# The order of the output matmuls' halves in a fused Fourier-mixing and feed-forward kernel

## The chip, the cores and the metric

The kernel runs on one core of one Trainium2 chip. The metric is device time in microseconds (us) of one launch. The core has five engines that matter here: TensorE (PE in the profile; PEld is its weight load), VectorE (DVE), ScalarE (ACT), GpSimd (POOL) and SyncE (SP), which issues the stores of the result.

## The reference

```
x: (8, 3008, 256) float32
X   = real(fft(fft(x, axis=1), axis=2))        # 8 sequences, 3008 positions, 256 features
t   = X.reshape(24064, 256)
h   = maximum(t @ w_in, 0)                     # w_in: (256, 2048)
out = (h * h) @ w_out                          # w_out: (2048, 256), out: (24064, 256) float32
```

So a two-dimensional Fourier transform of each sequence, of which the real part is kept, and then a feed-forward layer with a squared ReLU.

## The kernel before

The transform over the features is folded into the input weights once (`gh`). The transform over the positions is done with fold steps on VectorE (symmetric and antisymmetric sums of the sequence) and matmuls with cosine and sine tables (L486), whose results ScalarE and VectorE write as the columns `zc` and `zs` (L491, L495, L502). One column of these stands for a pair of output rows, k and its mirror image, and so gives two rows of the hidden layer.

**Windows and steps.** The columns are cut into 25 windows: 240, 512, 376, 376, 512, 448, then 512 each and a last one of 360. For each window the main loop goes through 8 steps (`s`, 0 to 7); a step makes 256 of the 2048 hidden units, that is two chunks of 128, for all columns of the window. The result is `h2`, of 16 chunks x 2 x columns, in float16, with two buffers, since the window after it reads it.

A step has one of two forms. In a plain step `pq` computes the sum of the two parts into a PSUM tile `ph` (L739, L740), `square` lets ScalarE apply the ReLU into `h1` (L749) and VectorE, or in some steps ScalarE, square it into `h2` (L754 or L752); then `turn` (L745) changes the sign of one part in `ph`, and ReLU and square are done again for the mirror rows. In a halved step `half_q` (L764) computes one part alone, ScalarE copies it to `sn` (L772), `half_p` (L778) adds the other part, ScalarE copies that to `hd` (L780), and for a group of one or two steps VectorE makes both signs from the copies: L788 and L792, then L802, L803 (the ReLU) and L804 (the squares, into `h2`). `PLAN` says which steps of a window are halved and where ScalarE squares. Step 0 is plain in every window. `ph` has two buffers, `h1` three.

**The output matmuls.** While window w makes its `h2`, the output of window w-1 is computed from the other `h2`, in `ffn2_steps`. Its rows are cut into groups of 128 (8 groups for 512 columns). A group needs 16 matmuls of 128 x 128 x 256 (L625), one for each chunk of `h2`, accumulated in PSUM; two groups share one bank of 512 float32 (`po`, two banks). The work of one group is given as two jobs, `part(i, 0)` with chunks 0 to 7 and `part(i, 1)` with chunks 8 to 15. The job that ends the second group of a bank also has ScalarE evict it (L640) into `osb` (three buffers) and SyncE issue its stores (L605).

`spread` deals the list of jobs over the 8 steps, two jobs a step for 8 groups; `others` issues them between the first and the second matmuls of a step (between `pq` and `turn`, or `half_q` and `half_p`), in this order with the fold work and the matmuls of the transform (L486):

```
for j in at[s]: j()                   # fold work of a later sequence
for j in spread(f2, s, NST): j()      # output matmuls of the window before
for j in post[s]: j()
...                                   # z: matmuls with the tables, L486
```

The order on each engine is the order in which the program issues the instructions (a manual schedule); waits between the engines are put in from what each instruction reads and writes. So the job list of `ffn2_steps` alone decides at which step a chunk of the older `h2` is first read. At the end of step 5 (in most windows) ScalarE issues a small DMA (L586), and at the end of a window its counterpart (L588), which bring a row into all partitions for L788.

Of the kernel before, what the change touches and what calls it, by code (L numbers as in the profile page):

```python
# [8 lines left out]
F32 = mybir.dt.float32  # L9
# [6 lines left out]
P = 128  # L16
# [12 lines left out]
def kernel(  # L29
# [14 lines left out]
    nc = tc.nc  # L44
    B, S, D = x.shape
# [8 lines left out]
    NFC = F // P  # L54
# [62 lines left out]
    ps_o = ctx.enter_context(tc.tile_pool(name="ps_o", bufs=2, space=bass.MemoryType.PSUM))  # L117
    ps_z = ctx.enter_context(tc.tile_pool(name="ps_z", bufs=2, space=bass.MemoryType.PSUM))
# [65 lines left out]
    wout16 = const.tile([P, NFC, D], F16, name="wout16")  # L184
# [405 lines left out]
    def store(osb, p0, g0, m, minus, eng=nc.sync):  # L590

        for b, k0, kstep, n, c0 in runs:
            il, ih = max(g0, c0) - c0, min(g0 + m, c0 + n) - 1 - c0
            if minus and k0 in (0, H):
                il = max(il, 1)
            cnt = ih - il + 1
            if cnt <= 0:
                continue
            if minus:
                lo = p0 + (m - 1) - (c0 + ih - g0)  # L600
                row = b * S + S - (k0 + kstep * ih)
            else:
                lo = p0 + c0 + il - g0
                row = b * S + k0 + kstep * il
            eng.dma_start(  # L605
                out=bass.AP(tensor=out.tensor, offset=out.offset + row * D, ap=[[kstep * D, cnt], [1, D]]),
                in_=osb[lo : lo + cnt, :])

    def ffn2_steps(w, h2, tail=False):

        g0, wn = wins[w]
        groups = [(q, min(P, 2 * wn - q)) for q in range(0, 2 * wn, P)]
        jobs = []
        st = {}

        def part(i, hf):
            q, m = groups[i]
            j = 0 if tail else i % 2
            if tail and hf == 0 and i % 4 > 1:
                st["po"] = ps_z.tile([P, 512], F32, name="po", tag="pz")  # L620
            elif j == 0 and hf == 0:
                st["po"] = ps_o.tile([P, 512], F32, name="po", tag="po")
            po = st["po"]
            for fc in range(hf * 8, hf * 8 + 8):
                nc.tensor.matmul(po[0:m, j * D : (j + 1) * D], h2[:, fc, q : q + m], wout16[:, fc, :], start=(fc == 0), stop=(fc == NFC - 1))  # L625
            if hf == 1 and tail:

                osb = osp.tile([P, 2, D], F32, name="osb", tag="osb")
                nc.scalar.activation(osb[0:m, 0, :], po[0:m, j * D : (j + 1) * D], AF.Copy, bias=0.0, scale=HS * HS)
                nu = max(0, min(m, wn - q))  # L630
                if nu:
                    store(osb[:, 0, :], 0, g0 + q, nu, False)
                if nu < m:
                    store(osb[:, 0, :], nu, g0 + 2 * wn - q - m, m - nu, True, nc.scalar if i % 2 else nc.sync)
            elif hf == 1 and (j == 1 or i + 1 == len(groups)):
                osb = osp.tile([P, 2, D], F32, name="osb", tag="osb")
                for a, b in ((i - j, i),) if j == 0 or m == P else ((i - 1, i - 1), (i, i)):
                    mm = groups[b][1]
                    lo, hi = (a % 2) * D, (b % 2 + 1) * D
                    nc.scalar.activation(osb[0:mm].rearrange("p s d -> p (s d)")[:, lo:hi], po[0:mm, lo:hi], AF.Copy, bias=0.0, scale=HS * HS)  # L640
                for b in range(i - j, i + 1):
                    q1, m1 = groups[b]
                    nu = max(0, min(m1, wn - q1))
                    if nu:
                        store(osb[:, b % 2, :], 0, g0 + q1, nu, False)
                    if nu < m1:
                        store(osb[:, b % 2, :], nu, g0 + 2 * wn - q1 - m1, m1 - nu, True)

        for i in range(len(groups)):
            for hf in range(2):  # L650
                jobs.append(lambda i=i, hf=hf: part(i, hf))
        return jobs

    def spread(jobs, i, n):
# [34 lines left out]
    for w in range(NW):  # L689
        g0, wn = wins[w]  # L690
        h2 = h2p.tile([P, NFC, 2 * WN], F16, name="h2", tag="h2")
# [37 lines left out]
        for u in need[w + 1]:  # L729
            zu = z_steps(u)  # L730
            zj += [(zu, 1, 0), (zu, 0, 0), (zu, 1, 1), (zu, 0, 1)]
        f2 = ffn2_steps(*old) if old else []
        phs = {}

# [117 lines left out]
    for j in ffn2_steps(*old, tail=True):  # L852
        j()
# [30 lines left out]
```

## Time and profile before

| | |
|---|---|
| median of 3 runs | 620.15 us (620.01 to 624.33) |
| the profiled execution | 619.85 us, of which 618.1 us are the span of the program's instructions |
| PE busy | 584.0 us (94%) |
| PEld busy | 421.0 us (68%) |
| DVE busy | 503.7 us (81%) |
| ACT busy | 519.1 us (84%) |
| output matmuls (L625) | 3024, busy 363.9 us, mean row 273 ns |
| idle time of PE ahead of them | 14.6 us |

A row of the profile gives the line, engine and operation, what it writes and reads, its count, then busy time and mean duration, and last the idle time of its engine before it and who ended most of that. The rows of matmuls overlap, since they are pipelined. In the timeline a line has start, duration, engine and source line, and in brackets the idle time of the engine before it with the instruction that ended it.

### The profile page before, as it was taken

The numbers are of one execution on the slowest core, as the hardware profiler recorded it, in microseconds if no ns is written. First come the engines' busy times: TensorE is split into PE (matmuls) and PEld (weight loads), VectorE is DVE, ScalarE is ACT, GpSimd is POOL, SyncE is SP. The second block draws the span as 40 slices with busy tenths as digits, with TensorE's granted clock in tenths as the row PEclk, the third lists the DMA queues.
The fourth block names the chain that finished last, engine by engine and source line by source line (L and its number), as shares of the span: only waits on it lengthen the run. The fifth ranks groups of instructions, "written<-read, shape, count | busy, mean of one in ns | idle before, by whom it ended". The sixth has DMA issues, their size and how long they took to land.

```text
span 618.1 us, 11384 instructions
## 1 busy us (share of the span) xinstructions
PE 584.0 (94%) x4386; PEld 421.0 (68%) x4386; DVE 503.7 (81%) x742; ACT 519.1 (84%) x673; POOL 85.3 (14%) x125
## 2 busy tenths in 40 slices
PE   5899999999998999998999989999899999999996
PEld 2457776776676677766776767767677676776685
DVE  7887677686988987989889889898798797887980
ACT  7786787889898889988888888988889898998881
POOL 5352200102001022030011200403000020000000
PEclk9999999999999999999999999999999999999999
DMA  8936121363114433432154311552111221221112
GB/s 146 218 74 141 56 72 35 57 139 104 53 49 85 119 100 83 112 110 58 50 102 104 98 53 43 103 125 83 51 35 61 86 70 49 56 51 50 49 55 66
DMA packets 39591, 50.20 MB, mean 81 GB/s; under 512 B 4572, under 2 KB 33393, under 8 KB 39537
## 3 DMA queue, kind: packets, MB, share of 16 engines
q0 software_dynamic: 9344, 22.14, 17.8%
q1 hardware_dynamic: 26899, 24.44, 12.9%
q10 hardware_dynamic: 3294, 2.90, 2.1%
q8 instruction: 34, 0.56, 0.4%
q14 instruction: 20, 0.16, 0.1%
HBM read 36.29 MB, written 27.86 MB: 104 GB/s over the span
## 4 chain that ended last, share of the span: by engine, by line
PE 45%; DVE 29%; issue 10%; ACT 10%; DMA 4%; POOL 1%; ACTq 0%; DVEq 0%; SPq 0%; POOLq 0%
PE po L625 27%; DVE h L804 7%; DVE hd L803 5%; DVE hd L802 5%; ACT h L749 4%; PE ph L745 4%; PE ph L778 3%; PE ph L764 3%; PE ph L739 3%; PE ph L740 3%; DMA out_dram<-osb 3%; DVE hd L788 2%; DVE h L754 2%; ACT sn L772 2%; DVE sn L792 2%
## 5 line engine op out<-in xcount | busy, mean ns | idle before, releaser
L625 PE MATMUL po<-wout,h 128*128 128x256 f16 (+1 forms) x3024 | 363.9, 273 | 14.6 <-DVE h L804 9.8
L625 PEld LDWEIGHTS <-h 128*128 128x128 f16 (+1 forms) x3024 | 295.6, 98 | 89.1 <-DVE h L804 11.7
L749 ACT ACTIVATE h<-ph 128x1024 f16<-128x1024 f32 (+4 forms) x222 | 204.8, 951 | 34.0 <-PE ph L745 13.7
L754 DVE TENSOR_TENSOR h<-h 128x1024 f16<-128x1024 f16 (+4 forms) x159 | 97.5, 632 | 38.9 <-ACT h L749 36.9
L804 DVE TENSOR_TENSOR h<-hd 128x4096 f16<-128x4096 f16 (+7 forms) x50 | 100.0, 1999 | 1.3
L780 ACT ACTIVATE hd<-ph 128x1024 f16<-128x1024 f32 (+3 forms) x89 | 89.1, 1001 | 12.3 <-PE ph L778 11.8
L772 ACT ACTIVATE sn<-ph 128x1024 f16<-128x1024 f32 (+3 forms) x89 | 88.8, 998 | 0.0
L792 DVE TENSOR_TENSOR sn<-sn,hd 128x2048 f16<-128x2048 f16 (+7 forms) x50 | 53.9, 1078 | 39.6 <-ACT sn L772 37.4
L739 PE MATMUL ph<-zc,gh 128*128 128x512 f16 (+4 forms) x222 | 79.6, 361 | 1.1 <-ACT h L749 0.8
L740 PE MATMUL ph<-zs,gh 128*128 128x512 f16 (+4 forms) x222 | 79.6, 361 | 0.4 <-ACT zs L495 0.4
L640 ACT ACTIVATE osb<-po 128x512 f32<-128x512 f32 (+3 forms) x95 | 54.6, 578 | 21.3 <-PE po L625 17.2
L752 ACT ACTIVATE h<-h 128x1024 f16<-128x1024 f16 (+3 forms) x63 | 64.8, 1029 | 2.0
L802 DVE TENSOR_TENSOR hd<-hd,sn 128x2048 f16<-128x2048 f16 (+7 forms) x50 | 53.8, 1076 | 12.4 <-ACT hd L780 10.6
L745 PE MATMUL ph<-zs,gh 128*128 128x512 f16 (+4 forms) x222 | 61.0, 361 | 2.2 <-ACT h L749 1.2
L803 DVE TENSOR_SCALAR hd<-hd 128x4096 f16<-128x4096 f16 (+7 forms) x50 | 54.0, 1080 | 1.4
L778 PE MATMUL ph<-zc,gh 128*128 128x512 f16 (+3 forms) x178 | 51.7, 371 | 2.0 <-ACT sn L772 2.0
L788 DVE TENSOR_SCALAR hd<-eb,wv 128x512 f16<-128x512 f16 (+3 forms) x178 | 51.6, 346 | 0.8 <-DMA eb<-zr 0.8
L764 PE MATMUL ph<-zs,gh 128*128 128x512 f16 (+3 forms) x178 | 51.7, 372 | 0.0
L740 PEld LDWEIGHTS <-gh 128*128 128x128 f16 x222 | 21.6, 98 | 23.7 <-issue 2.5
L739 PEld LDWEIGHTS <-gh 128*128 128x128 f16 x222 | 21.6, 97 | 22.4 <-DVE zc L502 0.5
L764 PEld LDWEIGHTS <-gh 128*128 128x128 f16 x178 | 17.3, 97 | 20.0
L429 POOL COPY xt<-xt 128x2 f16<-128x2 f16 x16 | 3.7, 262 | 174.2 <-DVE xt L412 156.3
(121 smaller groups left out, 392.0 us busy)
## 6 DMA issues: line engine op xcount, KB each, us to landing
out_dram<-osb SPq DMA_DIRECT2D x77, 128.0 KB
xo<-in_x_dram POOLq DMA_DIRECT2D x7, 768.0 KB
scr<-ev POOLq DMA_DIRECT2D x8, 390.0 KB, 4.5
eb<-zr ACTq DMA_DIRECT2D x18, 128.0 KB
rb<-scr POOLq DMA_DIRECT2D x16, 130.0 KB
out_dram<-osb SPq DMA_DIRECT2D x12, 94.0 KB
w<-in_moe_w_in_dram POOLq DMA_DIRECT2D x2, 512.0 KB
wout<-in_moe_w_out_dram POOLq DMA_DIRECT2D x1, 1024.0 KB
```

Source lines behind the costliest of these rows:

```text
L625: nc.tensor.matmul(po[0:m, j * D : (j + 1) * D], h2[:, fc, q : q + m], wout16[:, fc, :], start=(fc == 0), stop=(fc == NFC - 1))
L739: nc.tensor.matmul(ph[:, a, 0:wn], gh[:, 0, f0 : f0 + P], zcw[:, 0:wn], start=True, stop=False)
L740: nc.tensor.matmul(ph[:, a, 0:wn], gh[:, 1, f0 : f0 + P], zsw[:, 0:wn], start=False, stop=True)
L745: nc.tensor.matmul(phs[s][:, a, 0:wn], gh[:, 2, f0 : f0 + P], zsw[:, 0:wn], start=False, stop=True, skip_group_check=True)
L749: nc.scalar.activation(h1[:, :, 0:wn], phs[s][:, :, 0:wn], AF.Relu)
L754: return [lambda: nc.vector.tensor_tensor(h2[:, 2 * s : 2 * s + 2, sg * wn : (sg + 1) * wn], hv, hv, op=ALU.mult)]
L764: nc.tensor.matmul(ph[:, a, 0:wn], gh[:, 1, f0 : f0 + P], zsw[:, 0:wn], start=True, stop=True)
L772: nc.scalar.activation(sns[g][:, i : i + 2, 0:wn], ph[:, :, 0:wn], AF.Copy, bias=0.0, scale=-2.0)
L780: nc.scalar.activation(hds[g][:, i : i + 2, 0:wn], ph[:, :, 0:wn], AF.Copy, bias=0.0, scale=1.0)
L802: lambda: nc.vector.tensor_tensor(rev_dim(hd[:, :, wn : 2 * wn], 2), hd[:, :, 0:wn], sn[:, :, 0:wn], op=ALU.add),
L803: lambda: nc.vector.tensor_scalar(out=hv, in0=hv, scalar1=0.0, scalar2=None, op0=ALU.max),
L804: lambda: nc.vector.tensor_tensor(h2[:, 2 * g[0] : 2 * g[-1] + 2, 0 : 2 * wn], hv, hv, op=ALU.mult),
```

## The change

For the output of every window after the third (`w > 2`) but the last, the job list begins with the first halves of groups 0 to 3 and then has their second halves; groups 4 and up stay as they were. With 8 groups, steps 0 and 1 then run the chunks 0 to 7 of the groups 0, 1 and 2, 3, steps 2 and 3 their chunks 8 to 15, and steps 4 to 7 one whole group each. Both banks of `po` are open meanwhile, each with two unfinished groups. [...] The open tile is kept per group (`st[i]`) instead of in one name. The other functions are unchanged; lines behind the edit are 1 to 4 higher.

```
+        four = w > 2 and not tail
...
             if tail and hf == 0 and i % 4 > 1:
-                st["po"] = ps_z.tile([P, 512], F32, name="po", tag="pz")
+                st[i] = ps_z.tile([P, 512], F32, name="po", tag="pz")
             elif j == 0 and hf == 0:
-                st["po"] = ps_o.tile([P, 512], F32, name="po", tag="po")
-            po = st["po"]
+                st[i] = ps_o.tile([P, 512], F32, name="po", tag="po")
+            po = st[i - j]
             for fc in range(hf * 8, hf * 8 + 8):
-                nc.tensor.matmul(po[0:m, j * D : (j + 1) * D], h2[:, fc, q : q + m], wout16[:, fc, :], start=(fc == 0), stop=(fc == NFC - 1))
+                nc.tensor.matmul(po[0:m, j * D : (j + 1) * D], h2[:, fc, q : q + m], wout16[:, fc, :], start=(fc == 0 and (j == 0 or not four or i > 3)), stop=(fc == NFC - 1), skip_group_check=(four and i < 4))
...
-        for i in range(len(groups)):
-            for hf in range(2):
-                jobs.append(lambda i=i, hf=hf: part(i, hf))
+        order = [(i, hf) for i in range(len(groups)) for hf in range(2)]
+        if four:
+            order = [(i, hf) for hf in range(2) for i in range(4)] + order[8:]
+        for i, hf in order:
+            jobs.append(lambda i=i, hf=hf: part(i, hf))
         return jobs
```

## The prediction

> **What bounds the kernel now.** I read the page first, then the waits of TensorE (PE), then the timeline around two window starts.
>
> ```profile
> PE 584.0 (94%) x4386; PEld 421.0 (68%) x4386; DVE 503.7 (81%) x742; ACT 519.1 (84%) x673; POOL 85.3 (14%) x125
> ...
> PEclk9999999999999999999999999999999999999999
> ...
> L625 PE MATMUL po<-wout,h 128*128 128x256 f16 (+1 forms) x3024 | 363.9, 273 | 14.6 <-DVE h L804 9.8
> ```
>
> ```profile
> PE po L625 <- DVE h L804: 9.8, 7, 2.0
> PE po L625 <- DVE h L754: 4.8, 6, 1.0
> ...
> ACT h L749 <- DVE h L754: 11.8, 12, 1.9
> ```
>
> PE is busy 94% of the 618.1 us span, and its clock row is full. Its largest idle group, 14.6 us, is the output matmul L625, and the waits view (total us, times, longest) says for whom: for VectorE (DVE) to finish the last squares, 7 times L804 and 6 times L754. Those are the waits that the change aims at. The last row belongs beside them: ScalarE (ACT) waits for the same squares, 12 times, because `h1`, which its relu (L749) writes, has three buffers and a square (L754) must have read one before it is written again. The steady part repeats every three windows, and the windows view of one such period (386.46 to 460.62) has, in us and PE, PEld, DVE, ACT:
>
> ```profile
> sum 74.16, PE 71.31 PEld 51.38 DVE 64.75 ACT 64.92 POOL 12.69; mean PE 23.77 PEld 17.13 DVE 21.58 ACT 21.64 POOL 4.23
> ```
>
> PE stands still for 2.85 us of 74.16. DVE and ACT have 9 us of idle time each, but not at the window starts. This is the start of the window at 435.77, from the timeline (start, duration, engine, line; the bracket is the idle time before it):
>
> ```profile
> 436.39 1.93 ACT L749 ACTIVATE h<-ph 128x1024 f16<-128x1024 f32 x2
> 436.63 1.25 PE L625 MATMUL po<-wout,h 128*128 128x256 f16 x10
> 438.23 1.23 DVE L804 TENSOR_TENSOR h<-hd 128x2048 f16<-128x2048 f16 x1
> 438.35 1.06 ACT L752 ACTIVATE h<-h 128x1024 f16<-128x1024 f16 x1
> 439.37 1.28 DVE L754 TENSOR_TENSOR h<-h 128x1024 f16<-128x1024 f16 x2
> 439.51 0.83 PE L625 MATMUL po<-wout,h 128*128 128x256 f16 x6 [1.63 <-DVE h L804]
> 440.18 0.59 PE L745 MATMUL ph<-zs,gh 128*128 128x512 f16 x2
> 440.81 1.02 ACT L749 ACTIVATE h<-ph 128x1024 f16<-128x1024 f32 x1 [1.40 <-PE ph L745]
> 441.73 1.02 ACT L772 ACTIVATE sn<-ph 128x1024 f16<-128x1024 f32 x1
> 442.80 0.59 PE L778 MATMUL ph<-zc,gh 128*128 128x512 f16 x2
> ```
>
> Ten matmuls of group 0 run, the eleventh (its chunk 10) waits for the L804 square, which ends at 439.46. A matmul's row overlaps the next one's: ten take 1.25 us with 0.273 for the last, so they start 0.109 apart. So the eleventh was due at 437.72 and started 1.79 us late, 0.16 more than its idle time; with that for each of the 13 waits, 16.7 us are lost in all. I call this an L804 start (seven). An L754 start (six), at 410.40:
>
> ```profile
> 411.26 1.69 PE L625 MATMUL po<-wout,h 128*128 128x256 f16 x14
> 412.63 1.29 DVE L754 TENSOR_TENSOR h<-h 128x1024 f16<-128x1024 f16 x2
> 413.54 1.02 ACT L749 ACTIVATE h<-ph 128x1024 f16<-128x1024 f32 x1 [1.85 <-DVE h L754]
> 413.97 0.39 PE L625 MATMUL po<-wout,h 128*128 128x256 f16 x2 [1.01 <-DVE h L754]
> 414.20 0.48 PE L486 MATMUL pz<-sin,od 128*128 128x376 f16 x2
> 414.61 0.59 PE L745 MATMUL ph<-zs,gh 128*128 128x512 f16 x2
> ```
>
> Here the L754 square ends the wait of PE, and it also ends a wait of ACT: relu 0 of the new window starts at 413.54, ends at 414.56, and L745, which needs it, starts 0.05 us later.
>
> **The change, part by part.** *Work.* No instruction is added or removed on any engine: the same 16 matmuls of L625 stand in each step of a full window, in another order. In the built program the waits for L804 and L754 leave the first step; the one for the last L804 stands at the third block of 16, two steps later (a step is 2.7 us: 442.80 to 445.47 below, L778 to L778). A DVE that is 1.8 us late is not late there, so the 16.7 us at L625 go. The order of a step's other instructions and all DMAs stays; of stores only the first set per window is issued later, after its eviction.
>
> *Where the stall goes, L754 starts.* PE would reach L745 1.18 us sooner, at 413.43, but relu 0 still ends at 414.56, since it waits for DVE and not for PE. The stall of 1.18 moves from L625 to L745; gain 0. The six together were 4.8 + 6 x 0.16 = 5.8 us.
>
> *L804 starts.* Relu 0 (the second of the two at 436.39) is done at 438.32, so L745 moves to 438.39. Next, the second relu (440.81) needs L745 and, in the built program, also the first of the two L754 at 439.37, by the buffers of `h1`. That one ends at 439.37 + 0.69 = 440.06. So this relu moves to 440.10 and no further: 0.71 us. L772 follows 0.92 us after it and ends at 442.04; L778 needs it and starts at 442.09 instead of 442.80, where PE without any wait would have it at 441.01. Gain 0.71 of 1.79; the other 1.08 stand at L778, a wait "ACT sn L772". The first and the last of the seven, same reading:
>
> ```profile
> 191.29 1.29 DVE L754 TENSOR_TENSOR h<-h 128x1024 f16<-128x1024 f16 x2
> 192.73 1.02 ACT L749 ACTIVATE h<-ph 128x1024 f16<-128x1024 f32 x1 [1.70 <-PE ph L745]
> ...
> 583.80 1.28 DVE L754 TENSOR_TENSOR h<-h 128x1024 f16<-128x1024 f16 x2
> 585.11 0.77 ACT L749 ACTIVATE h<-ph 128x720 f16<-128x720 f32 x1 [1.19 <-DVE h L754]
> ```
>
> First: 192.73 - (191.98 + 0.04) = 0.71. Last: 585.11 - (584.48 + 0.04) = 0.59. Seven at 0.7 make 4.9 us.
>
> *The moved eviction.* Group pair 0/1 is now complete at the end of step 2 instead of step 1, so its L640 moves in ACT's queue: in the built program, 21 times, from ahead of the `hd` copy (L780) of step 1 to ahead of that of step 2. Queued behind it there are L491 (where a transform unit is due) and L780, and for L780 waits the DVE sum L802, the head of the run of squares that ends in L804 and L754 at the next window start. In the window that starts at 386.46 (steps 1 and 2):
>
> ```profile
> 392.09 0.60 ACT L640 ACTIVATE osb<-po 128x512 f32<-128x512 f32 x1
> 392.58 0.48 ACT L491 ACTIVATE es<-pz 128x377 f32<-128x377 f32 x1
> ...
> 394.70 0.24 PE L486 MATMUL pz<-cos,xt 128*128 128x188 f16 x1
> 395.15 0.49 ACT L491 ACTIVATE es<-pz 128x377 f32<-128x377 f32 x1 [0.26 <-PE pz L486]
> 395.58 1.02 ACT L780 ACTIVATE hd<-ph 128x1024 f16<-128x1024 f32 x1
> 396.64 1.23 DVE L802 TENSOR_TENSOR hd<-hd,sn 128x2048 f16<-128x2048 f16 x1 [0.49 <-ACT hd L780]
> ```
>
> An eviction holds ACT for 0.49 us (392.09 to 392.58) and can start 0.19 after the step's last output matmul gives way (394.70), so at 394.89, into idle time. It frees ACT at 395.38 where L491 started at 395.15: `hd` and L802 come 0.23 us later. In the two other windows of the period:
>
> ```profile
> 420.15 0.48 PE L486 MATMUL pz<-cos,od 128*128 128x376 f16 x2
> 420.67 0.48 ACT L491 ACTIVATE es<-pz 128x376 f32<-128x376 f32 x1 [0.44 <-PE pz L486]
> ...
> 445.47 0.59 PE L778 MATMUL ph<-zc,gh 128*128 128x512 f16 x2
> 446.10 1.02 ACT L780 ACTIVATE hd<-ph 128x1024 f16<-128x1024 f32 x1 [0.68 <-PE ph L778]
> ```
>
> By the same steps 420.34 + 0.49 - 420.67 = 0.16, and 445.66 + 0.49 - 446.10 = 0.05. From L802 to the next start DVE runs on without idle time, so these become delays of the 13 late starts: six L754 starts pay about 0.17 on the mean (most follow a window of the 0.23 kind), seven L804 starts about 0.14: 2.0 us. Bounds of this price: 0 per window where ACT was idle long enough, and the whole row, 0.60. I take 2.0, by the rows at the place itself. Step 1 loses the eviction, which lets its `hd` start up to 0.5 sooner; nothing waits for that one.
>
> *Buffers.* The output bank of groups 2/3 is opened at step 1 instead of 2. Its last eviction stands ahead of relu 0 in ACT's order, and L745 of step 0 waits for relu 0, so at step 1 PE finds the bank free. The bank that groups 4/5 need at step 4 is evicted at the end of step 2: a step of 2.7 us against 0.60. Cost 0; without that cover, 0.60 per window.
>
> *Sum.* 619.85 (the profiled execution's own time, span 618.1) - 4.9 + 2.0 = 616.95. The median of the runs lies 0.30 above that execution, so 617.2, 0.5% below 620.15.
>
> **The rivals.** *The stalls really go.* If the relu did not meet the `h1` wait, PE would be free: the seven L804 stalls are worth 9.8 + 7 x 0.16 = 10.9, so 609.0; with the other six, 603.1. For it speaks the page's idle time of DVE (19%); against it the 1.85 us row, where ACT is released by the same square as PE.
>
> *The eviction lengthens DVE's run (slower).* If ACT reaches the eviction of step 2 with no idle time, each costs its whole 0.60 ahead of L802. Then the seven gain 0.7 - 0.6 = 0.1 each, the six lose 0.6 each, and the eight remaining windows, where relu 0 ends within 0.1 us of need, lose 0.5: 619.85 - 0.7 + 3.6 + 4.0 = 626.8. It decides from the point where the idle time in front (0.26, 0.44, 0.68 in the rows above) is used up. Against it: those rows.
>
> *Nothing in total.* Gain and delay cancel: 620.
>
> *The clock.* At the kernel's start, before PE has run for long, matmuls go at half rate:
>
> ```profile
> 5.19 5.90 PE L309 MATMUL pw<-spn 128*128 128x384 f16 x20 [5.19 <-DVE spn L298]
> ...
> 11.25 1.14 PE L309 MATMUL pw<-spn 128*128 128x384 f16 x6
> ```
>
> That is 0.29 against 0.14 us per matmul, less the last one's tail. If PE fell back to it once in each of 21 windows for as long as those 20, it would cost 2.8 x 21 = 59 us, so 679. But behind the 1.63 us wait above six matmuls take 0.83 us, full rate, and the waits get shorter here, so I give it 1 in 100. [...]
>
> **How the numbers follow.** Forecast (0.7 gained at seven starts, about 0.15 paid at thirteen): 0.56, own range 614.9 (no delay) to 619.5. Stalls really go: 0.20. Slower by the eviction: 0.13. Nothing in total: 0.10. Clock: 0.01. 1% is about what a measurement of this kernel can tell from no change: under 613.9 or over 626.4. Faster 0.20, within 1% 0.66, slower 0.14. The range 608.5 to 626.0 takes in the delay's bound and 609.0, and leaves out the 603 end and the slow case, under 2 in 10.
>
> **What would show it.** Right: no wait of L625 for L804 or L754; at L754 starts L745 waits about 1.1 us for ACT L749; at L804 starts L778 of step 1 waits about 1 us for ACT L772; ACT L749 waits longer for L754 than 11.8 us; the period near 73.9 us against 74.16. Wrong: if these two waits stay short and the period falls to 72 us, the first rival holds; if L802 waits over 0.9 us for L780 and the period grows, the second does.

## The result, and the profile after

The changed kernel takes 618.32 us (median of 18 runs, 615.99 to 619.52), the kernel before 620.13 in the same measurement (619.22 to 624.42): ratio 0.995, 95% interval 0.9933 to 0.9967. So it is half a per cent faster, and the forecast was 617.2. From here on lines of the changed kernel carry its own numbers, 1 to 4 higher: L625 is L626, L745 is L749, L749 is L753, L754 is L758, L772 is L776, L778 is L782, L780 is L784, L802 is L806, L804 is L808.

The page of the changed kernel, its rows for the engines, the clock and the two matmul lines in question:

```profile
span 616.4 us, 11384 instructions
...
PE 585.2 (95%) x4386; PEld 421.9 (68%) x4386; DVE 503.8 (82%) x742; ACT 520.4 (84%) x673; POOL 84.4 (14%) x125
...
PEclk9899999999999999999999999999999999999999
...
L626 PE MATMUL po<-wout,h 128*128 128x256 f16 (+1 forms) x3024 | 361.7, 273 | 0.0
...
L782 PE MATMUL ph<-zc,gh 128*128 128x512 f16 (+3 forms) x178 | 51.7, 371 | 8.1 <-ACT sn L776 7.7
```

The output matmuls wait for nothing any more: 14.6 us of idle time before, 0.0 now. The work is the same. But PE's busy share rose by one point only: 8.1 us of idle time now stand at L782, where it was 2.0. The waits view (total us, times, longest) of the changed kernel:

```profile
PE ph L782 <- ACT sn L776: 7.7, 14, 1.5
PE pz L486 <- DVE od L383: 4.1, 6, 0.9
PE ph L749 <- ACT h L753: 2.7, 9, 0.5
...
ACT h L753 <- DVE h L758: 13.9, 17, 2.1
...
DVE hd L806 <- ACT hd L784: 15.8, 21, 1.0
```

Before, the same five rows were 2.0, 0.3, 1.2, 11.8 and 10.6 us. So 11.0 of the 14.6 us came back at three other lines of PE (5.7 + 3.8 + 1.5), each held by ACT or DVE.

The seven L804 starts went as the prediction worked them out. The timeline of the changed kernel behind the window start at 436.69 (before: 435.77):

```profile
437.55 1.91 PE L626 MATMUL po<-wout,h 128*128 128x256 f16 x16
439.27 1.23 DVE L808 TENSOR_TENSOR h<-hd 128x2048 f16<-128x2048 f16 x1
439.30 0.59 PE L749 MATMUL ph<-zs,gh 128*128 128x512 f16 x2
...
440.41 1.29 DVE L758 TENSOR_TENSOR h<-h 128x1024 f16<-128x1024 f16 x2
441.19 1.02 ACT L753 ACTIVATE h<-ph 128x1024 f16<-128x1024 f32 x1 [0.86 <-DVE h L758]
442.11 1.02 ACT L776 ACTIVATE sn<-ph 128x1024 f16<-128x1024 f32 x1
443.18 0.59 PE L782 MATMUL ph<-zc,gh 128*128 128x512 f16 x2 [1.10 <-ACT sn L776]
```

PE runs its sixteen matmuls in one piece and reaches L749 early. But the second relu (441.19) is now released by the first L758 square, for a buffer of `h1`, and L776 and L782 stand behind it. L782 comes 6.49 us after the window start where it came 7.03 after it: 0.54 gained of 1.79.

An L754 start, at 337.45:

```profile
338.75 1.47 PE L626 MATMUL po<-wout,h 128*128 128x256 f16 x12
339.67 1.29 DVE L758 TENSOR_TENSOR h<-h 128x1024 f16<-128x1024 f16 x2
...
340.88 0.18 DVE L383 CAST od<-py 128x6 f16<-128x6 f32 x1
341.11 0.49 PE L486 MATMUL pz<-sin,od 128*128 128x376 f16 x2 [0.89 <-DVE od L383]
341.53 0.59 PE L749 MATMUL ph<-zs,gh 128*128 128x512 f16 x2
```

Here the stall did not move to L749 but to a matmul of the transform ahead of it, L486, which needs a small cast that VectorE runs behind its two squares. Five of the six do this (windows 9, 11, 14, 17, 20); the sixth, window 7, waits 0.48 us at L749 for relu 0, as was forecast.

Window by window, from the first matmul of a window's step 0 to that of the next, in us (one profile each; groups of windows with the same pattern; of the last window, 24, to the end of its last matmul):

| windows | before | after | difference each |
|---|---|---|---|
| L804 starts 12, 15, 18 | 24.85 | 24.31 | -0.54 to -0.55 |
| L804 starts 8, 21, 23, 24 | 25.28, 23.97, 23.40, 31.82 | 24.80, 23.43, 22.80, 30.96 | -0.48 to -0.86 |
| L754 starts 7, 9, 11, 14, 20 | 24.20 to 25.46 | 24.16 to 25.43 | -0.03 to -0.05 |
| L754 start 17 | 25.37 | 25.57 | +0.20 |
| between them 10, 13, 16, 19, 22 | 23.63 to 24.22 | 23.84 to 24.40 | +0.12 to +0.21 |

Added up, the seven L804 starts gained 4.1 us, the six L754 starts nothing, and the five windows between lost 0.9.

The period of three windows that the prediction looked at (windows 16 to 18, 74.16 us) now takes 74.01, between its forecast of 73.9 and no change, because window 17 got longer. The period ahead of it, windows 13 to 15, gained more. Its sum row of the windows view (us, then PE, PEld, DVE, ACT, POOL), first of before, then of after:

```profile
sum 74.35, PE 71.45 PEld 51.45 DVE 64.65 ACT 64.90 POOL 8.55; mean PE 23.82 PEld 17.15 DVE 21.55 ACT 21.63 POOL 2.85
```

```profile
sum 73.94, PE 71.59 PEld 51.57 DVE 64.62 ACT 65.17 POOL 9.54; mean PE 23.86 PEld 17.19 DVE 21.54 ACT 21.72 POOL 3.18
```

The two profiled executions differ by only 1.7 us (619.85 and 618.14), less than the 3.4 us between the first window's start and the end. The rest is at the beginning: that of after reaches its first window 1.74 us later (23.48 against 21.74). The windows view of its first microseconds (length, then busy time and count of PE, PEld, DVE, ACT, POOL, then the granted clock of PE, DMA share and GB/s) says why:

```profile
14.00:16.00 2.00, 0.00 (x0) 0.00 (x0) 1.93 (x5) 0.54 (x1) 0.00 (x0) 0.95 1.04 177
16.00:18.00 2.00, 1.91 (x5) 0.73 (x6) 1.97 (x2) 0.00 (x0) 0.27 (x1) 0.50 1.19 203
18.00:20.00 2.00, 2.00 (x9) 0.90 (x8) 1.01 (x2) 1.42 (x2) 1.66 (x2) 0.70 1.44 197
```

At the end of a wait of 2.1 us for a load of weights (1.0 before) the granted clock fell to 0.50 for 3.41 us. That is the "8" in the clock row, in code that the change doesn't touch. It belongs to this execution; more on it below.

### The profile page after: what moved, and what is told of

Its sections match the earlier page's. It is cut to its first block, busy times and chain, and to the rows that moved or that the text cites. A ratio compares the mean times of both kernels' runs of the same rounds, so it can differ in the third digit from the quotient of the medians.

```text
span 616.4 us, 11384 instructions
## 1 busy us (share of the span) xinstructions
PE 585.2 (95%) x4386; PEld 421.9 (68%) x4386; DVE 503.8 (82%) x742; ACT 520.4 (84%) x673; POOL 84.4 (14%) x125
## 4 chain that ended last, share of the span: by engine, by line
PE 55%; DVE 19%; ACT 12%; issue 7%; DMA 4%; POOL 1%; ACTq 0%; SPq 0%; DVEq 0%; POOLq 0%
PE po L626 32%; ACT h L753 5%; PE ph L782 5%; PE ph L768 4%; DVE h L808 4%; PE ph L749 4%; PE ph L743 3%; PE ph L744 3%; PE pz L486 3%; DVE h L758 3%; DVE hd L806 3%; DVE hd L807 3%; DMA out_dram<-osb 3%; ACT sn L776 2%; ACT osb L641 2%
## 5 line engine op out<-in xcount | busy, mean ns | idle before, releaser
L626 PE MATMUL po<-wout,h 128*128 128x256 f16 (+1 forms) x3024 | 361.7, 273 | 0.0
L626 PEld LDWEIGHTS <-h 128*128 128x128 f16 (+1 forms) x3024 | 296.6, 98 | 71.2
L753 ACT ACTIVATE h<-ph 128x1024 f16<-128x1024 f32 (+4 forms) x222 | 205.0, 952 | 30.2 <-DVE h L758 13.9
L758 DVE TENSOR_TENSOR h<-h 128x1024 f16<-128x1024 f16 (+4 forms) x159 | 97.5, 632 | 35.0 <-ACT h L753 33.4
L808 DVE TENSOR_TENSOR h<-hd 128x4096 f16<-128x4096 f16 (+7 forms) x50 | 100.0, 1999 | 1.3
L784 ACT ACTIVATE hd<-ph 128x1024 f16<-128x1024 f32 (+3 forms) x89 | 89.1, 1001 | 13.3 <-PE ph L782 11.5
L776 ACT ACTIVATE sn<-ph 128x1024 f16<-128x1024 f32 (+3 forms) x89 | 88.6, 996 | 0.0
L806 DVE TENSOR_TENSOR hd<-hd,sn 128x2048 f16<-128x2048 f16 (+7 forms) x50 | 53.8, 1076 | 16.2 <-ACT hd L784 15.8
L749 PE MATMUL ph<-zs,gh 128*128 128x512 f16 (+4 forms) x222 | 61.1, 361 | 3.4 <-ACT h L753 2.7
L782 PE MATMUL ph<-zc,gh 128*128 128x512 f16 (+3 forms) x178 | 51.7, 371 | 8.1 <-ACT sn L776 7.7
L807 DVE TENSOR_SCALAR hd<-hd 128x4096 f16<-128x4096 f16 (+7 forms) x50 | 54.0, 1080 | 1.4
L792 DVE TENSOR_SCALAR hd<-eb,wv 128x512 f16<-128x512 f16 (+3 forms) x178 | 51.8, 347 | 1.9 <-DMA eb<-zr 1.9
L744 PEld LDWEIGHTS <-gh 128*128 128x128 f16 x222 | 21.6, 97 | 23.7 <-issue 2.5
L743 PEld LDWEIGHTS <-gh 128*128 128x128 f16 x222 | 21.6, 97 | 22.2 <-issue 0.5
L768 PEld LDWEIGHTS <-gh 128*128 128x128 f16 x178 | 17.2, 97 | 20.0
L749 PEld LDWEIGHTS <-gh 128*128 128x128 f16 x222 | 20.6, 97 | 11.3 <-issue 6.1
## 6 DMA issues: line engine op xcount, KB each, us to landing
w<-in_moe_w_in_dram POOLq DMA_DIRECT2D x2, 512.0 KB, 10.6
```

The source lines that it names most:

```text
L743: nc.tensor.matmul(ph[:, a, 0:wn], gh[:, 0, f0 : f0 + P], zcw[:, 0:wn], start=True, stop=False)
L744: nc.tensor.matmul(ph[:, a, 0:wn], gh[:, 1, f0 : f0 + P], zsw[:, 0:wn], start=False, stop=True)
L749: nc.tensor.matmul(phs[s][:, a, 0:wn], gh[:, 2, f0 : f0 + P], zsw[:, 0:wn], start=False, stop=True, skip_group_check=True)
L753: nc.scalar.activation(h1[:, :, 0:wn], phs[s][:, :, 0:wn], AF.Relu)
L758: return [lambda: nc.vector.tensor_tensor(h2[:, 2 * s : 2 * s + 2, sg * wn : (sg + 1) * wn], hv, hv, op=ALU.mult)]
L768: nc.tensor.matmul(ph[:, a, 0:wn], gh[:, 1, f0 : f0 + P], zsw[:, 0:wn], start=True, stop=True)
```

## The experiments

The first two take the change apart: one does the moved eviction alone, the other the reordered halves alone.

**The eviction alone.** The kernel before, with whole groups in the order 0, 2, 1, 3, so that the bank of 0/1 is complete and evicted in step 2, as in the change (with the tiles kept per group):

```
+        seq = list(range(len(groups)))
+        if w > 2 and not tail:
+            seq[1:3] = [2, 1]
-        for i in range(len(groups)):
+        for i in seq:
```

> The kernel before with the groups in the order 0, 2, 1, 3 and each group whole, so that only the first eviction moves: it stands ahead of the hd copy of step 2, as in the changed kernel, while group 0's second half stays in step 0 with its waits. My theory (the eviction delays the hd copy of step 2 and with it VectorE's run by 0.05 to 0.23 us, 2.0 us in all): 622 us, 0.3% slower than before; the waits of L625 for L804 and L754 stay near 14.6 us or grow by up to 2; VectorE's L802 waits 3 to 6 us longer for L780 in all than the 10.6 of before. Rival (the move costs nothing, and the changed kernel's gain is small only because of the wait for h1): 620.1 us. Rival (each eviction costs its whole 0.60 us): 627 us.

Measured: 622.41 us (620.44 to 625.38, 12 runs) beside 620.60, ratio 1.003 (1.0012 to 1.0049). Its waits (L804 is L807 here, L754 is L757, L802 is L805, L780 is L783):

```profile
PE po L625 <- DVE h L807: 10.4, 7, 2.2
PE po L625 <- DVE h L757: 4.8, 6, 1.0
...
DVE hd L805 <- ACT hd L783: 16.2, 21, 1.0
```

The wait of DVE for the `hd` copy grew from 10.6 to 16.2 us, as in the changed kernel (15.8), and the thirteen stalls stayed. In its profile windows 10, 13, 16, 19 and 22 are 0.12 to 0.22 longer, and 12, 15, 18 and 21 are 0.10 to 0.12 longer. Window 8 of this profile is 1.85 us longer; that was the clock (below), not the eviction. Without it the profile's windows are 1.2 us longer in all, and the medians differ by 1.8. So the price is real, and 1 to 2 us by this run; its better measure follows with the next one. Most of it is paid in the window of the eviction itself: step 4 of window 16 lasts 2.96 us instead of 2.77, since ACT comes 0.19 us late to the copy that this step's L781 waits for, and window 17 behind it starts no worse.

**The halves without the eviction.** The change with two groups interleaved instead of four, so that bank 0/1 is complete at the end of step 1, as before:

```
-            order = [(i, hf) for hf in range(2) for i in range(4)] + order[8:]
+            order = [(i, hf) for hf in range(2) for i in range(2)] + order[4:]
```

with the conditions on `start` and `skip_group_check` at `i > 1` and `i < 2`.

> The changed kernel with halves of groups 0 and 1 alone reordered (first halves of 0 and 1 in step 0, second halves in step 1), so that the first eviction stays in step 1, where it was before. My theory (gain 0.7 at each of seven starts, the price of the moved eviction gone): 615.2 us, 0.8% under before and some 2 to 3 us under the changed kernel; short waits of L626 for the last L808 in step 1, under 1 us in all; step 1's L782 waits about 1 us for L776 at seven starts. Rival (the second halves are needed too early at step 1, and the stall comes back there): 619 to 620 us, with several us of waits of L626. Rival (the eviction costs nothing): as the changed kernel.

Measured: 615.39 us (614.57 to 616.4, 6 runs), ratio 0.9915 (0.989 to 0.9939). Its waits:

```profile
PE po L626 <- DVE h L808: 0.2, 1, 0.2
...
PE ph L782 <- ACT sn L776: 6.3, 14, 0.9
PE pz L486 <- DVE od L383: 4.1, 6, 0.9
...
DVE hd L806 <- ACT hd L784: 10.8, 19, 0.8
```

One step's delay is enough for the squares: one wait of 0.2 us remains at L626, and the wait for `hd` is back at 10.8. The seven L804 windows are 0.68 to 0.91 shorter than before, 5.1 us in all (predicted 4.9), and windows 10, 13, 16, 19 and 22 have their old length. Window for window (4 to 24) the changed kernel is 2.0 us longer than this one: the eviction's price (predicted 2.0). This is the better version of the change.

**Four buffers for `h1`.** If the relu's wait for a buffer is what keeps the stalls, a fourth buffer sets them free in the changed kernel and does nothing in the one before. In both, one integer table moves to a pool of scratch tiles to make room:

```
-    h1p = ctx.enter_context(tc.tile_pool(name="h1p", bufs=3))
+    h1p = ctx.enter_context(tc.tile_pool(name="h1p", bufs=4))
```

The changed kernel:

> The changed kernel with four h1 buffers instead of three (an index tile of the start moves to another pool to make room). My theory (the gain stops at the relu that waits for a square to free an h1 buffer): the 1.2 us at the L754 starts and the other 1.1 at the L804 starts come too, 4 x 1.18 + 1.1 and 7 x 1.08, less some new lateness of VectorE: 606 to 610 us, 1.6 to 2.3% under before; ACT L753 hardly waits for DVE L758 (under 4 us in all against 13.9). Rival (VectorE's own lateness limits, and the buffer only shows it): 616 to 618 us, the waits at another line.

The kernel before:

> The kernel before with four h1 buffers. My theory (with the old order PE itself waits at L625 for the same squares, so the buffer alone frees nothing): 619 to 620.5 us, waits of L625 for L804 and L754 as before, 14 to 18 us. Rival (the buffer alone carries the gain, the order is beside the point): 608 to 614 us.

Measured: the changed kernel 609.81 us (609.67 to 611.16, 5 runs), ratio 0.9825 (0.9797 to 0.9852); the kernel before 623.58 (621.3 to 626.26, 12 runs), ratio 1.0039 (1.0017 to 1.006). The waits of the changed kernel with four buffers (lines one higher, in the kernel before too):

```profile
PE pz L487 <- DVE od L384: 4.4, 6, 0.9
PE ph L783 <- ACT sn L777: 2.2, 8, 0.4
PE ph L750 <- ACT h L754: 1.6, 7, 0.4
```

The wait at L783 fell from 7.7 to 2.2 us, the value of the kernel before (2.0), and no wait of the relu for a square is in its list, where it was 13.9. Windows 12, 15 and 18 are 1.52 us shorter than before: nearly the whole stall of 1.79 less the eviction. So the cap on the gain at these starts was the ring of three `h1` buffers. The L754 starts 11, 14 and 20 gained only 0.13 each, because L487 still waits for its cast, and 9 and 17 are 0.2 and 0.3 longer than before. The kernel before gained nothing, as expected, since its chunk order holds PE at the output matmuls whatever ACT does. That it got slower was not expected; its profile has the excess at two windows, 8 (+1.67) and 17 (+2.87), and in both the clock falls to half, at 191.18 and 416.46. At the second, ACT's relu first waits for a store of the result (timeline, and windows view):

```profile
415.65 1.02 ACT L750 ACTIVATE h<-ph 128x1024 f16<-128x1024 f32 x1 [3.25 <-DMA out_dram<-osb]
416.70 1.06 ACT L753 ACTIVATE h<-h 128x1024 f16<-128x1024 f16 x1
416.72 1.01 PE L746 MATMUL ph<-zs,gh 128*128 128x512 f16 x2 [1.04 <-ACT h L750]
```

```profile
416.00:418.00 2.00, 1.28 (x4) 0.44 (x4) 1.66 (x2) 1.96 (x3) 0.00 (x0) 0.61 0.89 182
```

**The cast one step earlier.** In the changed kernel the fold job with the cast L383 is issued in step 6 of the window before instead of step 7:

```
-            post[7] = fj[5:6]
+            post[6] = fj[5:6]
```

> The changed kernel with the fold's small matmul and cast (L381 to L383) one step earlier, at the end of step 6 instead of 7, so that the table matmuls L486 of the next window's step 0 need not wait for that cast. Theory (at the L754 starts three things come within 0.5 us of each other: the second half that the change moved away, the cast L383 and relu 0): the waits of L486 for L383 (4.1 us in the changed kernel) go, and about as much appears at L749 as waits for ACT L753, since relu 0 still waits for its h1 buffer; time within 0.7 us of the changed kernel's 618.3. Rival (the cast alone holds the L754 starts, the h1 buffer is beside the point there): 613 to 615 us.

Measured: 619.01 us (617.04 to 620.79, 10 runs), ratio 0.9971 (0.9952 to 0.999): no gain over the change. Its waits:

```profile
PE ph L749 <- ACT h L753: 6.5, 12, 1.1
...
PE pz L486 <- DVE od L383: 0.3, 1, 0.3
```

The stall at L486 fell from 4.1 to 0.3, and L749 took it over, 2.7 to 6.5, up to 1.1 at a time. (Window 5 is 1.07 us longer in this profile, with a wait of 0.9 at L381 in its step 6; the L754 starts differ from the changed kernel's by -0.25 to +0.08.) That is what the prediction had at the L754 starts: relu 0 ends just then too, so two waits lie on top of each other and removing one is worth nothing.

**Both limits at once.** Two groups with four buffers, without and with the earlier cast:

> Halves of groups 0 and 1 alone reordered, first eviction in step 1, and four h1 buffers. Theory: the 2 us of the moved eviction come off the 609.8 of four buffers with four groups, so 607 to 608.5 us, and the L754 starts still wait for L383 at L486 (4 to 5 us in all). Rival (without the h1 wait PE comes to the second halves of step 1 ahead of VectorE): 609 to 612 us, with waits of L626 for L808 of 3 us or more in all.

> As the run before with two groups and four h1 buffers, and the small matmul and cast of the fold at the end of step 6. Theory (with the second half, the h1 buffer and the cast all out of the way nothing holds PE at the L754 starts): 4 to 5 us less than with the cast late, 602.5 to 604.5 us, waits of L486 for L383 gone and no wait over 0.3 us at L749. Rival (VectorE's own lateness is passed on to a further wait at these starts): 606 to 608 us.

Measured: 611.32 us (609.6 to 611.64, 4 runs), ratio 0.9831 (0.9798 to 0.9864), and 607.37 (606.12 to 611.49, 4 runs), ratio 0.9797 (0.9751 to 0.9842). Both are about 3 us above the upper end of what was expected and inside the ranges of their rivals, but the waits that the rivals named did not come: L627 waits 0.2 us in each, and in the second PE waits for nothing at the starts 7, 9, 11, 14 and 20. The step between the two, 4 us, is the expected one: with four buffers the cast was the only thing left at the L754 starts (windows 11, 14, 20: 1.20 us shorter than before each; with the cast alone 0.03 longer, with the buffers alone 0.13 shorter). The first one's profile has the store's wait (3.5 us) and a fall of the clock to 0.50 at 410.44, in window 17 (+3.27), the second's has the wait (3.1 us) without the fall (+1.26) and loses 1.00 at window 5 to the earlier cast. The second's waits:

```profile
PE ph L750 <- ACT h L754: 3.4, 7, 2.4
...
ACT h L754 <- DMA out_dram<-osb: 3.1, 1, 3.1
```

**The row's DMA on another queue.** That wait has a small DMA of ACT's own just ahead of it (L588, the row for L788). I moved it to SyncE, in the kernel before, in the changed kernel, and in a version with all the gains so far:

```
-        row_back.append(lambda: nc.scalar.dma_start(...))
+        row_back.append(lambda: nc.sync.dma_start(...))
```

> The kernel before with the DMA of L588 issued by SyncE instead of ScalarE. What is asked: whether the runs above 621 us come from ScalarE's queue standing behind this issue, which waits at the window start near 411 us for the landing of an earlier store (413.01 in the profile of before, 413.94 of the changed kernel). Theory: the median falls by 0.5 to 1.5 us to 619 to 620 and the runs above 621.5 become rare. Rival (the high runs come from the first loads or from the end): the spread and the median stay. Rival (the row arrives later behind the stores, and VectorE's L788 waits for it): 621 us or more.

> The changed kernel with the DMA of L588 issued by SyncE instead of ScalarE. Theory: ScalarE no longer stands behind the landing of a store at the window start near 411, so 616.0 to 617.5 us against 618.3, and the same distance to the kernel before with the same edit as between the two kernels without it, some 3 us. Rival: no change, 618 to 619 us.

> All that held PE at the window starts taken away at once: two groups reordered with the first eviction in step 1, four h1 buffers, the fold's cast one step earlier from window 6 on, L588 on SyncE. Theory (the gains add): the 607.4 of the run with the first three less 1.0 for window 5 and up to 2 for ScalarE's DMA issue, so 603 to 605.5 us, 2.4 to 2.8% under before. Rival (SyncE's queue brings the row late, and VectorE's lateness comes back): 607 us or more.

Measured: 631.99 us (631.11 to 633.24, 6 runs), ratio 1.0179 (1.0153 to 1.0205); 625.65 (622.86 to 627.56, 11 runs), ratio 1.0073 (1.0048 to 1.0097); 615.15 (614.04 to 616.73, 6 runs), ratio 0.9905 (0.9879 to 0.9931). The first two lost to their counterparts, and the third, though faster than the kernel before, is 7.8 us behind nearly the same kernel with this DMA on ACT (607.37). The waits of the first:

```profile
DVE hd L788 <- DMA eb<-zr: 17.2, 9, 5.9
PE po L625 <- DVE h L804: 15.4, 9, 2.8
```

None of the three theories held. On SyncE the row is issued behind the stores of step 7, and it came late: in the first, L788 waits for it up to 5.9 us and 17.2 us in all, where it waited 0.8 us in the kernel before, and the squares behind it are late for PE. In the second the same line, L792 there, waits 20.9 us in all.

**The row's DMA earlier, on its own queue.** Two kernels: two groups, four buffers and the earlier cast (for windows after the fifth), and the same with the row's DMA issued ahead of step 7 instead of behind it:

```
+            while s0 == NST - 1 and row_back:
+                row_back.pop()()
```

> As the run with all of it, but L588 stays on ScalarE, where it was: two groups reordered, four h1 buffers, the fold's cast a step earlier from window 6 on. Theory (the gains at the starts add; window 5 gets its 1.0 back): 605.5 to 607.5 us, 2.1 to 2.4% under before, with one window near 411 us now and then 1 to 3 us long by ScalarE's wait for a store. Rival (VectorE takes back what PE gains, as with the late row): 609 us or more.

> As the run beside it, and the DMA of L588 issued by ScalarE ahead of step 7 of a window instead of after it, so that it does not stand behind the last stores of the window. Theory: the wait for a store at the window start near 411 goes, 604.5 to 606.5 us, half to one us under the run beside it. Rival (the small row of L586 has not landed a step earlier, and ScalarE waits for that instead): 607 to 612 us.

Measured: 608.98 us (605.87 to 610.04, 5 runs), ratio 0.9819 (0.9797 to 0.9842), and 605.52 (604.35 to 606.91, 5 runs), ratio 0.9759 (0.9736 to 0.9783), beside 619.78 for the kernel before. The first is 1.5 us above its range, the second inside its own. The waits of ACT in the last (L749 is L754 here, L629 is L631):

```profile
ACT h L754 <- DMA zr<-zs: 2.7, 3, 1.1
ACT osb L631 <- DMA out_dram<-osb: 2.0, 1, 2.0
```

The relu's wait for a store (3.4 us at window 17 in the first) is no longer there, and L631 is the end of the kernel. But ACT now stands still 1.7 us ahead of step 7 of window 16 and 1.1 us in window 18, and PE behind it at L750 (1.27 and 0.58 us, against 2.58 at window 17). So the wait was split and shifted more than removed, and the two profiled executions take the same time (605.87 and 606.01). The 3.5 us between the medians go with the granted clock, which was 0.989 to 1.0 in the runs of the first and 0.997 to 1.0 in those of the second; that the one long wait lowered the clock and the split one didn't would fit this, but was not tested. The second is the best version: 14 us, 2.4%, below the kernel before, where the change alone gave 0.5%.

## Why the prediction was right, and where not

*The stall leaves L625*: right, 14.6 us to 0.0, and L625 waits for neither square. No work was added; the row of L626 is 361.7 us against 363.9.

*L804 starts gain 0.7 of 1.79 each, before the eviction*: right in place and size. The halves alone gave 0.71 in most windows, 5.1 us for seven (predicted 4.9), the rest stands at L782 behind L776, and the fourth buffer, which takes away nothing but the relu's wait, released it (0.54 gained at 12, 15 and 18 with three buffers, 1.52 with four).

*L754 starts gain nothing, since the stall moves to L745 behind relu 0*: right in size, wrong in place. At five of the six it moved to L486 behind the cast L383. I had quoted that matmul at 414.20, between L625 and L745, and not asked what it reads: at 414.20 it followed the late L625 so closely that it showed no wait. The step left out was to recheck each instruction between the stall and the next known bound. It cost nothing here, because relu 0 was equally late, as the earlier cast alone showed (no gain, L749 at 6.5 us). It did cost the forecast for the four buffers its better end: there the two bounds come apart.

*The moved eviction costs 2.0 us at the thirteen late starts*: the size is right (2.0 by the windows of four groups against two; 1.8 by the medians of the eviction alone, 1.2 by its windows), the place is wrong for half of it. I took it that from L802 to the next start DVE runs on without idle time, and so let the whole delay arrive there. In fact PE itself meets it sooner, at step 4 of the same window, through the copies of ACT. The L754 starts paid none of the 0.17 each that I gave them; the five windows between paid 0.12 to 0.21 instead. By groups, L804 starts, L754 starts and windows between, the forecast was -3.9, +1.0 and 0, and measured are -4.1, 0.0 and +0.9 us: the two errors of place cancel in the sum, and that is luck.

*The sum*: -4.9 + 2.0 = -2.9. Measured -3.4 between the first window and the end of the profiles, and -1.8 between the medians. The median of after lies 1.1 above the forecast. At a mean granted clock of 0.998 or more, the 5 runs of after have a median of 616.51, and 29 runs of before, taken with the experiments, 619.72: -3.2.

*The clock*: the rival as I priced it (a fall in each of 21 windows, 679 us) did not come: the clock row of after is full behind its first microseconds, and the 3024 output matmuls, which now go over two banks twice per window, are busy 361.7 us against 363.9. (Two of its inputs were off: the fast matmuls at the start begin 0.16 us apart, (1.14 - 0.33) / 5, not 0.14; and a fall to 0.50 cost 1.67 us where it can be read off, below, not 2.8.) But my argument against it, full rate behind the 1.63 us wait, was drawn from one execution. The eviction's profile shows the same window start, with a wait of 2.18 us instead of 2.00, and the clock at half behind it. The windows view, the kernel before first, then the eviction alone:

```profile
190.00:192.00 2.00, 0.57 (x6) 0.52 (x7) 1.97 (x4) 1.03 (x1) 0.00 (x0) 1.00 0.37 101
192.00:194.00 2.00, 2.00 (x17) 1.42 (x15) 2.00 (x2) 1.27 (x2) 0.00 (x0) 1.00 0.00 0
```

```profile
190.00:192.00 2.00, 0.32 (x3) 0.30 (x4) 1.97 (x3) 1.06 (x1) 0.00 (x0) 0.98 0.41 114
192.00:194.00 2.00, 2.00 (x8) 0.96 (x7) 2.00 (x3) 0.15 (x1) 0.00 (x0) 0.50 0.00 1
194.00:196.00 2.00, 2.00 (x13) 1.37 (x12) 1.62 (x4) 1.79 (x2) 0.88 (x2) 0.67 0.00 0
```

8 matmuls where 17 ran. From the end of the wait to the third block of L625 the eviction alone takes 5.82 us (191.68 to 197.50), the kernel before 4.15 (191.43 to 195.58): 1.67 more, and with the wait 0.18 longer that is the 1.85 us of window 8. Within one execution the falls of the clock start on a grid of 3.413 us, and in these profiles it was the idle time of PE within one piece of that grid that went with a fall (last section).

*Other rivals*: "the stalls really go" needs the fourth buffer and the earlier cast, and then, with two groups, it holds for most of the gain (607.37; the rival had 603.1). The full price of the eviction did not come: L806 waits at most 1.0, and the period is no longer than before.

## What to carry to other kernels

When a wait is removed, list everything that the same late producer also holds (here a relu behind a ring of buffers and a tiny cast), and everything between the old stall and the next bound; the gain is the distance to the nearest of them, and lifting one of two that lie on top of each other shows nothing until the other goes too. Take the smallest version of a reordering: two interleaved groups hid the squares as well as four did (0.2 us of waits left), and moved no eviction. And look at which queue a small transfer shares: moving one behind the stores cost 11 us, part of it by falls of the clock (four in its profile, and the share is an estimate), where the matmul order gave 1.8.

## What the runs showed of the hardware that was not expected

*The scatter between these executions goes with the granted clock.* 61 executions of the kernel before, taken beside the experiments: the 29 with a mean granted clock of at least 0.998 have a median of 619.72 us (618.82 to 620.84), the 13 at 0.994 or less 622.83 (622.2 to 624.14). In the profiles a fall to 0.50 lasts 3.41 us (191.90 to 195.32 in the eviction alone); the one of the eviction alone cost 1.67 us. The slowest experiment, the row's DMA on SyncE in the kernel before, shows four such falls before its end, one of them twice as long, and a mean of 0.985: five lengths at 1.7 would be some 8 us, so much of its 11 us may be the clock and not the wait itself (an estimate). Where the executions without a profile lost their clock isn't known.

*In these profiles the clock falls on a grid.* The clock records of the traces give the start of each fall. In that slowest profile they are 192.03, 441.20, 492.40 and 594.80 us, which is 73, 15 and 30 times 3.413 us apart. In the seven other profiles with two starts or more (in most of them the last one comes behind the last matmuls) they are whole multiples of 3.413 apart too: 38, 58, 66, 125, 135 and 40, 174, 176. Cut each profile with such a start into pieces along its own grid, from where the clock first is full, and add up the time in each piece in which PE runs no matmul: all 13 falls ahead of the kernel's end come right behind a piece with 1.99 us or more, and no piece with 1.95 or less is followed by one. The length of a wait alone did not decide:

| profile | idle of PE | cut by the grid at | largest piece | fall |
|---|---|---|---|---|
| before, window 8 | 189.44 to 191.43 | 191.16 | 1.72 | none |
| before with four buffers, window 8 | 188.83 to 190.82 | not cut | 1.99 | 191.18 |
| the eviction alone, window 8 | 189.50 to 191.68 | not cut | 2.18 | 191.90 |
| four groups, four buffers, start | 13.52 to 15.52, and 0.78 up to 12.23 | 11.44 and 14.86 | 2.12 | 14.86 |

So a wait of 1.99 us brought no fall in one execution and one in another, and in the last row two waits of 0.78 and 1.34 us in one piece come ahead of a fall. A wait of 2.35 us, at window 17 of two groups with four buffers and the earlier cast (405.19 to 407.54), brought none; where the grid lies in that profile is not shown. All this is read off these profiles and was not tested by a run of its own; why one fall lasted two pieces (6.83 us from 492.40) is open.

*ACT stood behind a DMA that it issues itself.* At the start of window 17 (401 to 411 us) ACT waited 2.2 to 3.5 us for a store of the result to land, in the five profiles with four `h1` buffers in which ACT issues the row's DMA at the old place. In one of them, the kernel before with four buffers, the timeline shows that DMA (L589) issued at 415.19, right ahead of the relu at 415.65, which comes after 3.25 us of idle time. With the row's DMA issued a step sooner the wait at this place is gone and others come at windows 16 and 18 (1.7 and 1.1 us); why that DMA is tied to a store of SyncE's was not tested.
